# Two joined layers on one core: another order for the parameter stage of the convolution, and for the transposes of x

## The chip, the cores and the metric

The kernel runs on one core of a Trainium2 chip. The time is what the device takes for one execution, in microseconds (us), and a kernel's time is the median of its runs. A core has five engines that run their own queues of instructions in order: TensorE (PE in the profile; its weight loads are shown apart as PEld), VectorE (DVE), ScalarE (ACT), GpSimd (POOL) and SyncE (SP, which here only issues DMA transfers). Engines wait for one another by semaphores.

## The reference

Two layers that share nothing, their outputs side by side.

```
def _A_ref(x, mem0, Wq, Wk, Wv, Wo, seg_len):      # x 2048 x 1024, 32 heads of 128, memory 8 rows, seg_len 32
    mem = mem0
    for s in range(n_seg):                          # 64 segments, one after the other
        h = concatenate([mem, x[segment s]])
        q, k, v = h @ Wq, h @ Wk, h @ Wv            # per head
        p = softmax(where(mask, q @ k.T * scale, -1e9))
        o = (p @ v) @ Wo
        mem = o[:8];  outs.append(o[8:])

def _B_ref(u, A, B, C, log_dt, Dskip):              # u 2048 x 1024, D = 1024 channels, N = 128 states, complex
    dt = exp(log_dt)
    P = exp((dt * A)[:, :, None] * l)               # l = 0 .. 2047
    K = einsum('dn,dnl,dn->dl', C, P, dt * B).real
    y = irfft(rfft(pad(u)) * rfft(pad(K)))[:2048]   # length 4096
    return y + u * Dskip
```

Weights are bf16, x and u too; the output is 2048 x 2048.

## The kernel before, in words

`part_b` computes the second layer, and then `part_a` the first. Part A walks through the 64 segments, each of which needs the memory that the one before gave; it streams most of its weights from memory. What of a segment doesn't depend on the memory is worked out ahead, within part B, by the class `Ahead`: in every segment of 32 rows, the last 8 ("left rows", as they are what is left beside 24) get their keys, queries and values projected there (`projections`, 96 **slices**: 8 matmuls of 128x512 for keys and queries, L169, or 16 of 128x256 for values, L156, out of a transposed copy `xTl` of these rows; a slice ends with an eviction, L178 or L163, and stores to memory). The other 24 rows of a segment are only transposed and stored to `VXd`, for part A to read. Both come from `transposes`: 16 blocks of 128 rows, each loaded on POOL's queue, turned by eight PE transposes (L109) and copied by ACT into two places, the stage for `VXd` (L112) and `xTl` (L113). A slice's weights are 512 KB, loaded by SP into one of four buffers.

Part B's order is written out by hand. Its stages:

- **Parameter stage.** From A, B, C and log_dt, as 128x1024 f32 tiles, come for each state the logarithm of a modulus, a phase and a step's phase, in turns. Each goes to a scratch in memory (`PB`) as a sum of two or three bf16 parts (`put3`). `rows(q)` builds two small tables (RE, RT) on DVE. `matrices` makes the transform matrix MF (16 columns x cosine and sine x 512) by DVE and ACT: an angle by a product, its rounding by adding and subtracting a large number, then ACT's sine. The 16 blocks of x are turned in this stage, and 10 slices run. These pieces are generators, and `run` takes a step of each in turn.
- **Sixteen rounds**, by the string `ORDER`: in a round, eight pa matmuls (L1204) each followed by an exponential on ACT (L1212, E0 to E7), eight ptt matmuls (L1198) each followed by a rounding on DVE (L1220), two sines (L1225), two cosines (L1234), products on DVE (L1186, L1187) and a contraction on PE (L1016) that gives part of the kernel K, put to `Kd`. Beside that, words `P0` to `P5` start a slice, `p0` to `p5` evict it, and `U` words transform u (L975, with MF; its sums and differences on DVE, L986 and L987). ACT changes its function table twice a round. `classes` (L956 to L960) adds and subtracts pairs of those sums on POOL and stores them to `Ud` on POOL's queue. pa has one buffer. u is loaded in four quarters of its channels (`load_uq`), two ahead.
- **A transition**, with `build` (gf, L1137 and L1149; `make` steps it) and `weighted` (L1159), which make the tables of the transform of K.
- **Sixteen blocks** b, each a quarter of the channels (256) by a quarter of the frequencies: `spectrum(b + 1)` on PE (hps, L1175), the product with u's transform on DVE (`pointwise`, L1380 to L1386) into a buffer Bt, four blocks to a buffer. From block 4 on, `inverses` (yp, L1436) runs on PE, two for every block, with `ending` behind it. `load_u` and the loads of `MI`, the inverse's matrices, are on SP's queue. In blocks 1 to 14, `resident` loads those weights of part A that stay on the chip. At block 2, POOL forms a product of four rows with u's first rows (L1515), with the rows in a Bt buffer.

Tiles reuse buffers by tag: `kst` (one buffer of 128 x 8192 bf16, where keys and queries of a half are gathered), `wsl` (4), `B` (Bt, two pools), `mn` (two buffers for the inverse's products).

Of the kernel before, what the change touches and what calls it, by code (L numbers as in the profile page):

```python
# [12 lines left out]
I32 = mybir.dt.int32  # L13
# [61 lines left out]
class Ahead:  # L75
# [19 lines left out]
    def transposes(self, pool, ps, ident):  # L95
        nc = self.nc
        def load(b):
            xb = pool.tile([128, self.Dm], BF16, name="xb", tag="xb")
            nc.gpsimd.dma_start(out=xb[:], in_=self.x[b * 128:(b + 1) * 128, :])
            return xb  # L100
        xbs = [load(b) for b in range(3)]
        yield
        for b in range(self.S // 128):
            if b + 3 < self.S // 128:
                xbs.append(load(b + 3))
            xb = xbs[b]
            pt = ps.tile([128, self.KC, 4, self.SL], BF16, name="pt_x", tag="ptx")
            for kc in range(self.KC):
                nc.tensor.transpose(out=pt[:, kc, :, :].rearrange("p a b -> p (a b)"), in_=xb[:, kc * 128:(kc + 1) * 128], identity=ident[:])  # L109
            yield  # L110
            xst = pool.tile([128, 4, self.KC, self.XM], BF16, name="xst", tag="xst")
            nc.scalar.copy(out=xst[:].rearrange("p s k r -> p k s r"), in_=pt[:, :, :, 0:self.XM])  # L112
            nc.scalar.copy(out=self.xTl[:, :, 4 * b:4 * b + 4, :], in_=pt[:, :, :, self.XM:self.SL])  # L113
            nc.sync.dma_start(out=self.VXd[4 * b:4 * b + 4, :, 256:].rearrange("s p f -> p s f"), in_=xst[:].rearrange("p s k r -> p s (k r)"))
            yield
# [545 lines left out]
ON_DVE = (('p1', 'P', 1), ('p4', 'P', 4), ('u0', 'U', 1), ('u1', 'U', 3), ('m', 'M', 0))  # L661


def part_b(ctx, tc, u, A_re, A_im, B_re, B_im, C_re, C_im, log_dt, Dskip, out_b, ahead, copies, residents, first_state):
# [10 lines left out]
    PB = [dram.tile([PARTS[q], 8, 128, 128], BF16, name="PB%d" % q) for q in range(2)]  # L675
# [27 lines left out]
    with tc.tile_pool(name="b_par", bufs=1) as par, tc.tile_pool(name="b_parh", bufs=2) as parh, tc.tile_pool(name="b_mg", bufs=2) as mg, \  # L703
            tc.tile_pool(name="a_prx", bufs=4) as prx, tc.tile_pool(name="a_ppt", bufs=4, space=PSUM) as ppt:
        ldt = par.tile([128, 8], BF16, name="ldt")
        sy.dma_start(out=ldt[:], in_=log_dt.rearrange("(t p) -> p t", p=128))
        nat = {}
        for nm, src in (("Cr", C_re), ("Ci", C_im), ("Br", B_re), ("Bi", B_im), ("Ai", A_im), ("Ar", A_re)):
            nat[nm] = par.tile([128, 8, N], BF16, name="nat" + nm)
            sy.dma_start(out=nat[nm][:], in_=src.rearrange("(t p) n -> p t n", p=128))  # L710
        dtb = par.tile([128, 8], BF16, name="dtb")
        sc.activation(out=dtb[:], in_=ldt[:], func=ACT.Exp)
        sh = [128, 8, N]

        def f32(name):
            return par.tile(sh, F32, name=name)

        def put3(x, q, row):
            hi = parh.tile(sh, BF16, name="hi", tag="hi")
            sc.copy(out=hi[:], in_=x[:])  # L720
            sy.dma_start(out=PB[q][row].rearrange("t p n -> p t n"), in_=hi[:])
            yield
            v.tensor_tensor(out=x[:], in0=x[:], in1=hi[:], op=ALU.subtract)
            mid = parh.tile(sh, BF16, name="mid", tag="mid")
            sc.copy(out=mid[:], in_=x[:])
            sy.dma_start(out=PB[q][row + 1].rearrange("t p n -> p t n"), in_=mid[:])
            yield
            lo = parh.tile(sh, BF16, name="lo", tag="lo")
            v.tensor_tensor(out=lo[:], in0=x[:], in1=mid[:], op=ALU.subtract)
            sy.dma_start(out=PB[q][row + 2].rearrange("t p n -> p t n"), in_=lo[:])  # L730
            yield

        def run(*gens):
            gens = list(gens)
            while gens:
                for g in list(gens):
                    if next(g, g) is g:
                        gens.remove(g)

        ci = mg.tile([128, 512], I32, name="ci", tag="ci", bufs=1)  # L740
        gp.iota(ci[:], pattern=[[2, 512]], base=1, channel_multiplier=0)
        ri = mg.tile([128, 4, 4], I32, name="ri", tag="ri", bufs=1)
        gp.iota(ri[:], pattern=[[1, 4], [512, 4]], base=0, channel_multiplier=4)
        colk = mg.tile([128, 512], F32, name="colk", tag="colk", bufs=1)
        v.tensor_copy(out=colk[:], in_=ci[:])
        v.tensor_scalar(out=colk[:], in0=colk[:], scalar1=float(1.0 / (2 * PLEN)), scalar2=None, op0=ALU.mult)
        rowl = mg.tile([128, 16], F32, name="rowl", tag="rowl", bufs=1)
        v.tensor_copy(out=rowl[:], in_=ri[:].rearrange("p a b -> p (a b)"))

        def some(g, n):  # L750
            for _ in range(n):
                next(g, None)
                yield

        def sines(c, cs):
            return MF[:, :, c:c + 2, cs, :].rearrange("p k c n -> p c k n")

        def columns(tm):
            return tm[:].rearrange("p c (k n) -> p c k n", k=4)

        def matrices():

            tms, kMs = {}, {}
            for c in range(0, 20, 2):
                if 4 <= c:
                    tm = tms.pop(c - 4)
                    v.tensor_scalar(out=tm[:].bitcast(I32), in0=tm[:].bitcast(I32), scalar1=0x7FFFFFFF, scalar2=None, op0=ALU.bitwise_and)
                    sc.activation(out=sines(c - 4, 0), in_=columns(tm), func=ACT.Sin, scale=-TWO_PI, bias=hp[:])
                if 2 <= c < 18:
                    tm = tms[c - 2]  # L770
                    v.scalar_tensor_tensor(out=tm[:], in0=kMs.pop(c - 2)[:], scalar=MAGIC, in1=tm[:], op0=ALU.subtract, op1=ALU.subtract)
                    sc.activation(out=sines(c - 2, 1), in_=columns(tm), func=ACT.Sin, scale=-TWO_PI)
                if c < 16:
                    tms[c] = mg.tile([128, 2, 512], F32, name="tm", tag="tm", bufs=4)
                    for i in range(2):
                        v.tensor_scalar(out=tms[c][:, i], in0=colk[:], scalar1=rowl[:, c + i:c + i + 1], scalar2=None, op0=ALU.mult)
                    kMs[c] = mg.tile([128, 2, 512], F32, name="mkM", tag="mkM")
                    sc.activation(out=kMs[c][:], in_=tms[c][:], func=ACT.Identity, bias=magic[:])
                yield

        dt_b = dtb[:].unsqueeze(2).to_broadcast(sh)
        mats = matrices()
        for _ in range(2):
            next(mats)


        jI = par.tile([128, NE + NA], I32, name="jI")
        o = 0
        for b0, st, n in FINE + COARSE + TURNS:
            gp.iota(jI[:, o:o + n], pattern=[[st, n]], base=b0, channel_multiplier=0)  # L790
            o += n
        jF = par.tile([128, NE + NA], F32, name="jF")
        v.tensor_copy(out=jF[:], in_=jI[:])
        pI = par.tile([128, 2], I32, name="pI")
        gp.iota(pI[:, 0:1], pattern=[[1, 1]], base=0, channel_multiplier=1)
        v.tensor_scalar(out=pI[:, 1:2], in0=pI[:, 0:1], scalar1=3, scalar2=None, op0=ALU.bitwise_and)
        pF = par.tile([128, 2], F32, name="pF")
        v.tensor_copy(out=pF[:], in_=pI[:])
        tI = par.tile([128, 8], I32, name="tI")
        gp.iota(tI[:], pattern=[[1, 8]], base=0, channel_multiplier=0)  # L800
        tF = par.tile([128, 8], F32, name="tF")
        v.tensor_copy(out=tF[:], in_=tI[:])
# [18 lines left out]
        own, lo, hi_ = rows(0)  # L821
        jE = par.tile([128, NE], F32, name="jE")
        v.tensor_scalar(out=hi_, in0=lo, scalar1=-1.0, scalar2=1.0, op0=ALU.mult, op1=ALU.add)
        v.tensor_scalar(out=jE[:, 0:NF], in0=jF[:, 0:NF], scalar1=lo, scalar2=None, op0=ALU.mult)
        v.tensor_scalar(out=jE[:, NF:], in0=jF[:, NF:NE], scalar1=lo, scalar2=hi_, op0=ALU.mult, op1=ALU.add)
        v.tensor_tensor(out=RE[:], in0=bcast_mid(own[:], NE), in1=bcast_front(jE[:], 8), op=ALU.mult)
        own, lo, hi_ = rows(1)
        jT = par.tile([128, NT], F32, name="jT")
        ang = par.tile([128, 1], F32, name="ang")
        v.scalar_tensor_tensor(out=ang[:], in0=lo, scalar=-1.0, in1=hi_, op0=ALU.add, op1=ALU.add)  # L830
# [80 lines left out]
        for i in range(9):  # L911
            next(mats, None)
            evict_next = next(pro)
            evict((sc.copy, v.tensor_copy)[i % 2])
            evict = evict_next
# [779 lines left out]
```

## Time and profile before

| | |
|---|---|
| median of 3 runs | 2008.63 us (2002.54 to 2014.86) |
| profiled execution | 2001.01 us, of which the span of the profile is 1999.3 us |
| mean granted PE clock | 0.971 |
| busy: PE, DVE, ACT, POOL | 1831.9, 1413.8, 960.1, 416.9 us |
| DMA | 588.69 MB, mean 294 GB/s |
| first exponential of round 0 (L1212) | 103.23 us |
| first sine of rounds 0, 1, 2 (L1225) | 115.80, 135.74, 156.20 us |
| a round after that | 19.95 us |
| first pointwise product (L1380) | 436.09 us |
| first matmul of the inverse (L1436) | 496.80 us |

All times within an execution count from the span's start. A share of busy time is a mean over stages with different limits, so the table of windows, below, is read stage by stage. Matmuls are pipelined and their ends are modelled: a busy PE is not a PE at its peak, and the time from one group's start to the next's says more than a group's length.

### The profile page before, as it was taken

What the parts mean: (1) busy time and instruction counts of PE and PEld (TensorE: products, weight loads), DVE (VectorE), ACT (ScalarE), POOL (GpSimd) and SP (SyncE); (2) the same over time, 40 slices, a digit from 0 to 9 for tenths busy, and PEclk for the clock granted to TensorE, in tenths of its full rate; (3) what the DMA queues carried; (4) which work ended last, traced back from release to release, by engine and by line L of the source; (5) the groups of instructions that cost most, each with busy time, mean ns of one, the idle gap of its engine ahead of it and who ended that gap; (6) DMA issues with size and microseconds to landing.
All of it is one profiled execution on the core that took longest, in us unless ns stands there. A gap on an engine that the chain in (4) does not pass through costs nothing.

```text
span 1999.3 us, 74588 instructions
## 1 busy us (share of the span) xinstructions
PE 1831.9 (92%) x31956; PEld 1131.2 (57%) x31956; DVE 1413.8 (71%) x3441; ACT 960.1 (48%) x1673; POOL 416.9 (21%) x851
## 2 busy tenths in 40 slices
PE   1589999978999799999999999999999999999999
PEld 1365766645888455555555555555555555555554
DVE  8779999988995366666666666666766666666650
ACT  4888989872223243434343434444343444444330
POOL 2126454533100011111111111111111111111120
PEclk9699999977999899999999999999999999999999
DMA  6688997748768999999999999999999999999991
GB/s 173 179 229 266 266 267 204 193 117 278 216 203 260 328 327 340 341 331 349 340 340 335 351 337 342 346 342 349 348 348 342 337 347 340 349 342 349 344 339 42
DMA packets 348484, 588.69 MB, mean 294 GB/s; under 512 B 109880, under 2 KB 225928, under 8 KB 346104
## 3 DMA queue, kind: packets, MB, share of 16 engines
q1 hardware_dynamic: 294764, 526.35, 78.0%
q10 hardware_dynamic: 44812, 28.26, 4.6%
q0 software_dynamic: 8576, 29.32, 4.2%
q8 instruction: 250, 4.10, 0.8%
q14 instruction: 82, 0.67, 0.1%
HBM read 528.25 MB, written 66.05 MB: 297 GB/s over the span
## 4 chain that ended last, share of the span: by engine, by line
PE 39%; DMA 21%; DVE 3%; issue 1%; ACT 1%; POOL 0%; SPq 0%; DVEq 0%; POOLq 0%
PE acc L376 23%; DMA wst<-WD_v 8%; PE pp L489 8%; DMA wst<-WD_o 7%; PE pe L626 3%; PE tr L387 2%; DMA wst<-WD_k 2%; DMA arena<-PKd 2%; DMA wst<-WD_q 2%; PE pv L457 1%; DVE arena L583 1%; PE sc L401 1%; PE pv L461 1%; ACT arena L583 1%; PE tro L589 1%
## 5 line engine op out<-in xcount | busy, mean ns | idle before, releaser
L376 PEld LDWEIGHTS <-a_hT 128*32 128x32 bf16 x12352 | 328.0, 96 | 313.6 <-issue 57.0
L382 ACT CAST arena<-acc 128x512 bf16<-128x512 f32 x384 | 225.1, 586 | 393.9 <-PE acc L376 314.6
L489 PEld LDWEIGHTS <-arena 128*32 128x32 bf16 x8256 | 216.3, 96 | 86.9 <-issue 62.5
L376 PE MATMUL acc<-wst,a_hT 128*32 128x512 bf16 x2304 | 230.2, 382 | 23.9 <-DMA wst<-WD_v 20.5
L390 POOL COPY arena<-arena 128x128 bf16<-128x128 bf16 x128 | 37.3, 292 | 825.0 <-DMA arena<-PKd 277.9
L297 DVE TENSOR_SCALAR arena<-keep 128x256 int32<-128x256 int32 (+1 forms) x512 | 175.7, 395 | 27.6 <-PE acc L376 27.2
L376 PE MATMUL acc<-XM,a_hT 128*32 128x512 bf16 x2560 | 185.9, 381 | 0.0
L169 PE MATMUL pro<-XM,wsl 128*128 128x512 bf16 x512 | 119.5, 389 | 10.4 <-ACT XM L113 8.1
L489 PE MATMUL pp<-W_o,arena 128*32 128x256 bf16 x3584 | 122.8, 274 | 4.7 <-DMA W_o<-in_A_Wo_dram 4.6
L416 DVE TENSOR_REDUCE a_mx<-sc 128x4 f32<-128x160 f32 (+1 forms) x192 | 71.7, 374 | 74.9 <-PE sc L404 74.9
L420 ACT ACTIVATE sc<-sc 128x160 f32<-128x160 f32 (+1 forms) x192 | 63.9, 333 | 125.5 <-DVE sc L417 124.9
L376 PE MATMUL acc<-W,a_hT 128*32 128x512 bf16 x1536 | 119.4, 382 | 0.1
L504 DVE COPY arena<-tr 128x512 bf16<-128x512 bf16 x64 | 27.2, 425 | 126.8 <-PE tr L387 126.8
L424 DVE TENSOR_REDUCE a_mx<-sc 128x4 f32<-128x160 f32 (+1 forms) x192 | 72.8, 379 | 55.5 <-ACT sc L420 55.2
L1212 ACT ACTIVATE E<-pa 128x648 bf16<-128x648 f32 x128 | 91.1, 711 | 29.2 <-PE pa L1204 24.1
L1436 PE MATMUL yp<-Bt,MI 128*128 128x256 bf16 x680 | 104.5, 273 | 0.0
L376 PE MATMUL acc<-g,a_hT 128*32 128x512 bf16 x1024 | 102.6, 382 | 0.0
L451 POOL TENSOR_TENSOR arena<-arena,a_BD 128x128 bf16<-128x128 bf16 x128 | 51.1, 399 | 236.8 <-DVE arena L434 232.4
L583 ACT CAST arena<-pp 128x128 bf16<-128x128 f32 x64 | 17.0, 266 | 160.2 <-DVE arena L583 160.2
L489 PE MATMUL pp<-wst,arena 128*32 128x256 bf16 x1536 | 76.5, 275 | 17.3 <-DMA wst<-WD_o 14.4
L169 PEld LDWEIGHTS <-wsl 128*128 128x128 bf16 x512 | 51.1, 100 | 72.9 <-issue 18.5
L376 PE MATMUL acc<-wq,a_hT 128*32 128x512 bf16 x1024 | 91.4, 382 | 0.0
(338 smaller groups left out, 4100.2 us busy)
## 6 DMA issues: line engine op xcount, KB each, us to landing
wst<-WD_v SPq DMA_DIRECT2D x256, 512.0 KB
wst<-WD_k SPq DMA_DIRECT2D x192, 512.0 KB
wst<-WD_o SPq DMA_DIRECT2D x192, 512.0 KB
wst<-WD_q SPq DMA_DIRECT2D x128, 512.0 KB
Ud<-ux POOLq DMA_DIRECT2D x16, 1024.0 KB, 5.9
wq<-Ud SPq DMA_DIRECT2D x32, 512.0 KB
wsl<-in_A_Wk_dram SPq DMA_DIRECT2D x16, 512.0 KB
wsl<-in_A_Wv_dram SPq DMA_DIRECT2D x16, 512.0 KB
```

The costliest lines, as they stand in the source:

```text
L169: nc.tensor.matmul(a[:], lhsT=w[:, kc, 128 * j:128 * j + 128], rhs=xTl[:, kc, :, :].rearrange("p s k -> p (s k)"), start=(kc == 0), stop=( ...
L297: nc.vector.tensor_scalar(out=out.bitcast(I32), in0=in_.bitcast(I32), scalar1=0, scalar2=None, op0=ALU.bitwise_or)
L376: nc.tensor.matmul(a[32 * g:32 * g + 32, o_:o_ + rhs.shape[1]], lhsT=hT[:, kc, :], rhs=rhs, start=(kc == 0), stop=(kc == KC - 1), tile_pos ...
L382: nc.scalar.copy(out=q, in_=a[:])
L416: nc.vector.tensor_reduce(out=m_, in_=x, axis=AX.X, op=ALU.max)
L420: nc.scalar.activation(out=flat(sc, i), in_=flat(sc, i), func=ACT.Exp, scale=scale)
L424: nc.vector.tensor_reduce(out=m_, in_=x, axis=AX.X, op=ALU.add)
L489: nc.tensor.matmul(po[32 * qt:32 * qt + 32, o_:o_ + rhs.shape[1]], lhsT=oT[:, h % 4, (h % 16) // 4, :], rhs=rhs, start=False, stop=(h == 3 ...
L583: (nc.scalar.copy if j else nc.vector.tensor_copy)(out=osb[:, 128 * j:128 * j + 128], in_=pp[:, 1, 128 * j:128 * j + 128])
L626: nc.tensor.matmul(pe[n][:], lhsT=left[2 * b + hi // 16][:, 128 * (hi % 16):128 * (hi % 16) + 128], rhs=wo[u][:, 1024 * hh + 512 * n:1024 ...
L1212: sc.activation(out=T["E", r, e // 4][:, lo:lo + 8 * NE].rearrange("p (i c) -> p i c", i=2), in_=T.pop(("p", r, e))[:, :, 0:4 * NE], func= ...
L1436: pe.matmul(yp[:, b, :], lhsT=m_[:, b, cs, kc, :], rhs=Bt[:, kc, j, half, c_, :], start=(kc == 0 and cs == 0 and half == 0), stop=(kc == 3 ...
```

## The change

1. **Parameter stage.** It becomes one list of words (`PAR`), worked off in order. Of x only the left rows are read, in four loads, turned 16 segments at a time (words T), and copied into `xTl` by ACT (c) or DVE (C). The angles of MF come from PE: two 7-row tables of small bf16 numbers, turned by 24 transposes, and 32 matmuls of 128x512 (F) whose result is taken as the low 16 bits of a PSUM word, so that ACT's sine (f) reads turns. The modulus goes by logarithm and exponential, and the angle by an arctangent of a ratio; there is no reciprocal. Eight products of 128x1024 are on POOL (Wi1, Wi2, Wi, pr, s1, s6, lo1, lo6). Channels lie on partitions as (p t) in place of (t p), so a partition's piece of a parameter or of PB is 2 KB in one run; loads are split between SP's and ACT's queues. 21 slices (P, evicted on DVE, d, or ACT, e) run here.
2. **Rounds.** From round 3 on, the word P4 does nothing: five slices a round. A quarter of u is asked for one ahead, at the second of the four steps of the quarter before; the second buffer first holds the 7-row tables of the parameter stage.
3. **Transition.** The last `classes` runs on DVE, ahead of the second half of the first spectrum; it was on POOL, at the end.
4. **Half blocks.** The other 24 rows are turned in blocks 1 to 4 of the sixteen: 3, 5, 6 and 2 blocks of 96 rows, behind that block's spectrum. Loads are on POOL's queue, two blocks to a buffer of tag `mn`, two such pairs ahead; a further pair is loaded when a pair's second block has been copied. ACT copies into ten places of a buffer of tag `B`, and SP stores to `VXd`. The four rows of block 2 move to another tile, and `resident` loads start at block 2.

```
+    def left_rows(self):
+        held = self.pool.tile([128, 4, 2048], BF16, name="xl", tag="kst")
...
+            self.nc.gpsimd.dma_start(out=xb, in_=x_s[16 * i:16 * i + 16, self.XM:self.SL, :])
...
+    def other_rows(self, two, stage, bank, ident):
...
+            t_ = two()
+            for i in range(2):
+                b = blocks.pop(0)
+                xb = t_[0:n, 1024 * i:1024 * i + 1024]
+                nc.gpsimd.dma_start(out=xb, in_=x_s[4 * b:4 * b + 4, 0:self.XM, :])
+                xbs.append((b, xb))
+        load()
+        load()
         yield
...
+        while xbs:
+            b, xb = xbs.pop(0)
+            pt = bank()[:, :, 0:n]
             for kc in range(self.KC):
...
+                nc.tensor.transpose(out=pt[:, kc, :], in_=xb[:, 128 * kc:128 * kc + 128], identity=ident[0:n, 0:n])
+            xst = stage()
+            nc.scalar.copy(out=xst.rearrange("p s k r -> p k s r"), in_=pt.rearrange("p k (s r) -> p k s r", r=self.XM))
+            nc.sync.dma_start(out=self.VXd[4 * b:4 * b + 4, :, 256:].rearrange("s p f -> p s f"), in_=xst.rearrange("p s k r -> p s (k r)"))
+            if b % 2 and blocks:
+                load()
             yield
...
+PAR = ("F0 Wr2 T0 T1 T2 F1 f0 T3 F2 c2 C1 c0 Wr1 C3 a2 f1 F3 P0 f2 t1 Wr F4 sq1 d0 Wi1 P1 Wi2 t2 f3 F5 f4 d1 t3 a1 P2 Wi m f5 pr F6 P3 d2 "
+         "sq2 F7 P4 mx f6 d3 sm hi1 P5 d4 P6 f7 p lnm P7 lns q4 d5 ex t4 F8 P8 e6 F9 ra d7 xr at t5 P9 d8 b1 f8 f9 hi2 F10 f10 F11 d9 s1 f11 "
+         "mi1 b2 P10 F12 F13 d10 f12 f13 P11 hi4 b3 F14 d11 F15 P12 q3 F16 f14 hi6 f15 F17 s6 hi3 s4 P13 f16 d12 F18 f17 s3 mi4 F19 lo1 f18 "
+         "d13 P14 s2 mi3 F20 F21 d14 f19 f20 lo3 rt P15 F22 f21 F23 F24 mi6 d15 F25 lo6 f22 mi2 f23 f24 P16 lo4 F26 lo2 rp f25 f26 F27 d16 "
+         "F28 f27 F29 f28 P17 F30 F31 f29 f30 f31 P18 e17 e18 P19 e19 P20 e20").split()
...
+            "Wi1": tt(gp, W_im, nat["Cr"], nat["Bi"], MU), "Wi2": tt(gp, y2, nat["Ci"], nat["Br"], MU), "Wi": tt(gp, W_im, W_im, y2, AD),
...
+            "pr": tt(gp, x3, W_re, W_im, MU), "ra": tt(v, x3, x3, x5, MU), "at": act(x3, x3, ACT.Arctan),
...
+            "rp": powers_rows, "rt": phase_rows}
+        for k, x, eng in (("1", x1, gp), ("2", x2, v), ("6", x6, gp), ("4", x4, v), ("3", x3, v)):
+            par_ops.update({"hi" + k: high(k, x, 0), "s" + k: rest_(eng, k, x), "mi" + k: high(k, x, 1), "lo" + k: lowest(eng, k, x)})
...
+            pe.matmul(mt[:], lhsT=turns_l[:, i // 2, :], rhs=turns_r[:, i % 2, :], start=True, stop=True)
...
+                sc.activation(out=MF[:, :, i // 2, i % 2, :], in_=mt[:].bitcast(I16)[:, 0:1024:2].rearrange("p (k n) -> p k n", k=4), func=ACT.Sin,
+                              scale=float(TWO_PI / 65536))
...
-        uvs = [load_uq(0), load_uq(1)]
+        uvs = [load_uq(0)]
...
+                if kc == 1 and dq < 3:
+                    uvs.append(load_uq(dq + 1))
...
-                            sums.append(lambda: classes(kc, dq, got[2], s_))
+                            sums.append(lambda: classes(v, kc, dq, got[2], s_))
...
+            elif nm == "P4" and f > 2:
+                continue
...
     weighted(0, 1, amps[0])
+    sums.pop()()
     spectrum(0, 1, [t_[:, 0] for t_ in now[1]])
...
+    others = ahead.other_rows(two, stage, lambda: banks[-1](), ident)
+    next(others)
     for b in range(16):
         dq = b // 4
+        if b == 4:
+            for _ in others:
+                pass
...
-            rows4 = bp.tile([128, 4, 2, 2, 2, DQ], BF16, name="r4", tag="B")[0:4, 0, 0].rearrange("p a b c -> p (a b c)")
+            rows4 = g0[0:4, 5120:6144]
...
-        for _ in range({1: 2, 2: 2, 3: 1, 4: 2, 5: 2, 6: 2, 7: 1, 11: 3, 12: 3, 13: 2, 14: 3}.get(b, 0)):
+        for _ in range({1: 3, 2: 5, 3: 6}.get(b, 0)):
+            next(others)
+        for _ in range({2: 1, 3: 2, 4: 3, 5: 3, 6: 2, 7: 1, 11: 3, 12: 3, 13: 2, 14: 3}.get(b, 0)):
             next(resident)
```

Lines that the list leaves out as "..." are the small tables, the products of the parameter stage and the loads of its inputs, which the words above tell.

More of the change, by code (lines that the diff above doesn't have):

```diff
@@ L758, in columns @@
[L758 to L779, printed above, removed]
```

348 lines of the change are left out of this document (177 added, 171 removed).

## The prediction

> **What bounds the kernel now.** I read the page's strip of 40 slices first (50 us each; a digit is the busy share in tenths), to find the stages.
>
> ```profile
> PE   1589999978999799999999999999999999999999
> ...
> DVE  8779999988995366666666666666766666666650
> ACT  4888989872223243434343434444343444444330
> POOL 2126454533100011111111111111111111111120
> PEclk9699999977999899999999999999999999999999
> ```
>
> Slices 1 and 2 are the parameter stage: TensorE (PE) nearly empty, its clock down to 0.6, VectorE (DVE) and ScalarE (ACT) full. Slices 3 to 8 are the sixteen rounds, 9 and 10 the first half blocks, and from slice 11 on PE is full to the end. So a microsecond taken ahead of slice 10 counts whole only if nothing between gives it back. Then the busy times by window (columns: window, length, then PE, weight loads, DVE, ACT and POOL busy with instruction counts, clock, DMA share, GB/s):
>
> ```profile
> 0.00:25.00 25.00, 4.06 (x32) 3.18 (x33) 21.26 (x54) 8.13 (x8) 9.32 (x31) 1.00 0.86 210
> 25.00:50.00 25.00, 3.97 (x32) 3.39 (x32) 22.04 (x17) 15.55 (x19) 2.41 (x4) 0.93 0.54 136
> 50.00:75.00 25.00, 7.23 (x64) 5.93 (x64) 20.19 (x22) 18.91 (x31) 3.98 (x6) 0.57 0.84 210
> 75.00:103.00 28.00, 25.67 (x99) 10.70 (x99) 21.54 (x34) 26.47 (x29) 5.60 (x27) 0.84 0.56 151
> ...
> 254.00:274.00 20.00, 20.00 (x242) 11.61 (x241) 18.68 (x30) 17.91 (x21) 10.22 (x13) 1.00 1.07 275
> ...
> 474.00:497.00 23.00, 17.45 (x124) 13.42 (x124) 22.86 (x21) 1.89 (x4) 10.19 (x32) 0.85 0.84 281
> 497.00:650.00 153.00, 151.80 (x1368) 131.64 (x1367) 126.69 (x149) 46.78 (x52) 7.68 (x20) 1.00 0.72 227
> ```
>
> DVE bounds the parameter stage up to 75 us, ACT and PE after it. The first exponential of the rounds (L1212, "E0" below) starts at 103.23 us. DVE bounds the last of the first half blocks (22.86 of 23). The inverse (yp, L1436) starts on PE at 496.80 and keeps PE full until part A. These two times, **E0 and the inverse's start**, are my yardsticks.
>
> **Parameter stage.** Removed are the 128x1024 products that made the transform's angles on DVE and ACT, a reciprocal of 6.55 us (L885) and 24 of every 32 transposed rows. Left, by rows of this profile:
> - DVE: 23 steps of 128x1024 f32 at 1.14 us (26.2), 2 with a scalar at 0.60, 17 evictions at 0.60 (10.2), 2 PSUM copies at 0.68, the two row builders at 2.45 and 3.3, some 20 small ones at 0.13: 48 us.
> - ACT: 8 functions at about 1.0, 10 casts at 0.95, 32 sines out of PSUM at 0.52 (16.6), five evictions at 0.57, three turn copies at 0.98, two xTl copies at 0.7, some 8 table loads at 1.28: 52 us.
> - PE: 21 slices at 1.73 (24 matmuls took 5.18), 32 angle matmuls at 0.27, 56 transposes at 0.13 cold: 52 us.
>
> Three engines with about 50 us each, against 85 on DVE before. PE's slices can't begin until the left rows are transposed and copied. A load of x lands about 5 us after issue here, and four pieces must be issued, landed, transposed (1.03 each) and copied (0.7): I put the first slice at 14.2, an estimate. From there PE has 36.3 (slices) + 8.6 (angles) + 1.7 (the first slice cold: 64 cold matmuls took 16.61), and about 5 for ptt, table load and pa ahead of E0: 66. The word list delays some slices behind the two row builders on DVE: 70. **Floor of the gain: E0 at 70, −33.**
>
> Eight 128x1024 products go to POOL. This trace shows what that does beside DVE (start, length, engine, line):
>
> ```profile
> 447.88 6.30 DVE L1159 TENSOR_TENSOR XM<-XM 128x1536 bf16<-128x1536 bf16 x1
> ...
> 448.08 1.28 POOL L956 TENSOR_TENSOR ux<-us 128x512 f32<-128x512 f32 x1
> 449.33 1.29 POOL L957 TENSOR_TENSOR ux<-us 128x512 f32<-128x512 f32 x1
> 450.59 2.77 POOL L959 TENSOR_TENSOR ux<-us 128x256 f32<-128x256 f32 x4
> ```
>
> A DVE product that takes 0.95 us elsewhere ends only when POOL's products have ended; at 486.37 an L1383 of 1.22 took 2.38 beside POOL's L1515. By L956, eight of twice its width take 8 x 2.57 = 20.6 us. DVE works in order, so evictions queue behind a blocked product, and PE behind them. With 48 us of work in some 55, DVE takes about half of the 20.6 as delay: E0 at 79, **−24**. All of it would be E0 at 86 to 90, −17 to −13.
> The Trainium skill, "SBUF — State Buffer", section on who interferes with whom, has a VectorE instruction with two SBUF inputs and a GpSimd one that reads SBUF exclude each other for whole instructions. L1159's 6.30 agrees; by that rule alone, all of the 20.6 would be paid only if no other VectorE work were free to run.
>
> The first load of u for the rounds is now behind seven stores on SP's queue, and the first ups matmul of round 0 waits for it; between 0 and 3.8 us, I take **+3.5** (it sits behind the last eviction).
>
> **Rounds.** Twelve rounds lose P4 (8 or 16 matmuls, 1.73 us of PE) and its eviction (0.68 of DVE). What sets a round's 19.95 us is seen on ACT (idle before in brackets):
>
> ```profile
> 272.63 0.71 ACT L1212 ACTIVATE E<-pa 128x648 bf16<-128x648 f32 x1 [0.63 <-PE pa L1204]
> 273.87 0.71 ACT L1212 ACTIVATE E<-pa 128x648 bf16<-128x648 f32 x1 [0.53 <-PE pa L1204]
> 274.60 1.28 ACT L1225 ACT_TABLE_LOAD   x1
> 275.89 1.72 ACT L1225 ACTIVATE sn<-nr 128x1824 bf16<-128x1824 f32 x1
> ```
>
> PE reads 100% busy, but the waits for pa are those of a single pa buffer: exponential, matmul, exponential. P4 stands behind the last pa, beside E7, the table load and the sines. DVE, too, meets the sines with 0.2 us in hand. So I take 0.13 a round, **−1.6**; bounds 0 and the whole 1.73 a round (−21).
>
> **Between rounds and blocks.** The last class products go from POOL to DVE: 2.4 us there by 1.14 for a step of 1024, while DVE has 5 us idle in 418:436. L1159's extra 5.35 goes; PE lost 1.85 right behind it, then 0.54. What is late next is the following coefficient load, at about 447. I take **−2.5** (0 to −5.3).
>
> **The other 24 rows of x in the first half blocks.** Added in blocks 1 to 4, ahead of the inverse: 16 loads on POOL's queue, 128 transposes on PE, 16 copies of 0.69 to 0.81 on ACT, which is idle (1.89 of 23), and 16 stores on SP ahead of the next load of u. PE's queue gets them in order: 24 transposes ahead of the fourth spectrum, 40 ahead of the fifth, 64 ahead of the sixth, then the inverse.
> - Transposes: eight take 0.45 to 0.62 warm and 1.03 cold, so 16 blocks cost 7 to 16.5; I take 10.
> - Loads: two pairs of blocks ahead, a further pair issued only when a pair is used. A pair needs 2 x 0.6 of issue and 5.0 to land. The wait of a pair that was not issued early is about 5 less the transposes beside it. I find two such on PE (blocks 6 and 7, blocks 12 and 13), and POOL's own product (L1515) ahead of the third pair: +10.
> - Stores: SP's loads of u(4) and u(5) queue behind five and eight stores, and Bt of the fifth block reuses the buffer the stores read: +2, with a colder PE:
>
> ```profile
> 486.39 6.21 PE L1175 MATMUL hps<-XM,g 128*128 128x256 bf16 x40 [2.45 <-DVE y L1380]
> 492.43 4.53 PE L1175 MATMUL hps<-XM 128*128 128x256 bf16 x40
> ```
>
> - Cover: PE is idle for 9 us between 436 and 497, and DVE is the bound of its last 23; I credit 4, as most of that idle time lies ahead of where the transposes go.
>
> That is **+18**: 10 + 10 + 2 − 4. The lower bound is 8 (transposes in idle time, one wait), the upper 28 (transposes cold, 16.5; waits 10; 2 for stores, no cover). After the inverse starts PE is full, so none comes back. The weights that part A keeps are loaded one block later: free, as the DMA share there is 0.72.
> The Trainium skill, "TensorE: Matmul & The Clock Gate", Part 4, says that transposes don't count as busy for the clock. The granted 0.57 in 50:75, where PE did little else, agrees. By that rule all three spectra of blocks 3 to 5 would run cold, as rival 3 has them.
>
> **Sum**, against the profiled execution (2001.01 us, span 1999.3, 1.7 around it): −24 + 3.5 − 1.6 − 2.5 + 18 = −6.6, so 1994.4 for one like it. The median shown, 2008.63, is 0.38% above that execution; on its scale **2002**.
>
> **Rivals.**
> 1. *POOL's products find DVE elsewhere and the x rows are mostly covered.* For: eight POOL products in a 60 us stage, DVE evictions read PSUM; against: 6.30 beside 0.95. E0 at 70, rows at +8 to +12: −33 + 3.5 − 1.6 − 2.5 + 10 = −23.6, **1985** in the median's scale. Chance 0.22.
> 2. *PE is the bound of the rounds after all* (it reads 20.00 of 20): 12 x 1.0 to 1.73 off on top of my sum, −17 to −26: **1982 to 1991**. Against: ACT's single-buffer waits. Chance 0.09.
> 3. *Slower: the chain of x loads sets the half blocks.* If each of the six later pairs waits out its 6.2 us on PE's in-order queue (37), with transposes cold (16.5) and the spectra cold too (three of 40 at 8.0 for 4.53, by 20 in 4.02: 10), less 9 of idle: +54, in place of +18: **2038**. It decides from about +44 on, where it outweighs the −24 by 1%. For: two buffers only, loads issued behind POOL's own products; against: the loads are for the next block, and spectra lie between. Chance 0.13.
> 4. *The change doesn't shorten the parameter stage as it says*: DVE blocked for all of 20.6, E0 at 88, −15 in place of −24: **2011**, inside the forecast's band. Chance 0.14.
>
> My own case has 0.42. **Faster by over 1%** (about what a measurement of this kernel can tell from no change: its runs spread by 0.6%): rivals 1 and 2, 0.31. **Slower by over 1%**: rival 3 and 0.01 of rival 4, 0.14. **Within**: the rest, 0.55. The range leaves out the far end of rival 2 and rival 3: downwards −33 + 0 − 1.6 − 2.5 + 8 = −29, and 2 of rival 2's smallest share: 1977; upwards −15 + 3.8 + 0 + 0 + 28 = +17: 2025.
>
> **What would show it.** E0 at 79 (70: rival 1; 88: rival 4), with DVE products of 2 to 4 us beside POOL's. Sines 19.8 us apart (18.5: rival 2). The inverse at about 490, 17 us behind where E0's gain alone puts it (rival 3: over 50), PE waiting for loads of xb in two places. The forecast is most likely wrong in how much of POOL's 20.6 DVE pays, and in how many x loads PE waits for.

## The result, and the profile after

The changed kernel takes **2058.93 us** (median of 4 runs, 2053.86 to 2063.03) against 2005.59 us of the kernel before in the same comparison: a ratio of **1.0264**, 95% interval 1.0227 to 1.0301. It is slower by 53 us, where 2002 was forecast and 2025 was the end of the range. Its profiled execution took 2063.03 us (span 2061.3), the slowest of the four.

The page's strip for the changed kernel (40 slices of 51.5 us, busy share in tenths; last line the DMA engines):

```profile
PE   7699999783599879989999999999999999999999
...
DVE  7499989874399446666766666566666666667650
...
PEclk8899999866699979999999999999999999999999
DMA  6869975646567889999999999999999999999991
```

PE is now busy in the first two slices, as the change wants. The hole has moved to slices 10 and 11, from about 464 to 567 us, which lie in the half blocks. The same by windows (window, length, then PE, weight loads, DVE, ACT, POOL busy with counts, clock, DMA share, GB/s):

```profile
25.00:50.00 25.00, 24.87 (x108) 9.38 (x107) 23.47 (x27) 22.36 (x27) 3.97 (x2) 1.00 0.52 151
...
254.00:274.00 20.00, 18.74 (x275) 14.75 (x274) 17.93 (x30) 17.89 (x21) 9.31 (x12) 1.00 0.91 246
...
480.00:500.00 20.00, 4.51 (x36) 3.30 (x35) 2.21 (x2) 3.20 (x4) 6.02 (x8) 0.50 0.30 77
500.00:520.00 20.00, 6.62 (x56) 5.14 (x54) 6.98 (x6) 2.40 (x3) 1.96 (x3) 0.67 0.72 205
520.00:540.00 20.00, 3.28 (x32) 2.44 (x32) 0.00 (x0) 3.20 (x4) 3.38 (x10) 0.50 0.41 116
```

In the stretch from 480 to 540 no engine is busy for half of the time, and DMA is at 0.30, 0.72 and 0.41: something is being done one at a time. The times that part the stages:

| us from the span's start | before | after | difference | each stage's own |
|---|---|---|---|---|
| first exponential of the rounds, E0 | 103.23 | 83.22 | −20.0 | −20.0 |
| first sine | 115.80 | 101.05 | −14.75 | +5.25 |
| last sine | 418.43 | 405.32 | −13.1 | +1.65 |
| first matmul of the inverse | 496.80 | 549.90 | +53.1 | +66.2 |

From the inverse to the end this execution took 1511.4 us, and before 1502.5. In ten of the eleven edited kernels below that last part took 1496 to 1510, so the 9 us are within what executions differ by (the eleventh, e11 with 1517, has a reason of its own, given there); the 53.1 ahead of it is the whole difference of the medians.

What happened from 480 to 545 is seen when PE's queue and POOL's are laid side by side. PE first (start, length, engine, line, what, idle before and what ended it):

```profile
504.47 0.51 PE L134 MATMUL yp<-b_ident,xb 96*128 96x96 bf16 x8
511.41 0.82 PE L134 MATMUL yp<-b_ident,xb 96*128 96x96 bf16 x8 [6.44 <-DMA xb<-in_A_x_dram]
516.82 0.82 PE L134 MATMUL yp<-b_ident,xb 96*128 96x96 bf16 x8 [4.58 <-DMA xb<-in_A_x_dram]
522.26 0.82 PE L134 MATMUL yp<-b_ident,xb 96*128 96x96 bf16 x8 [4.62 <-DMA xb<-in_A_x_dram]
...
543.83 0.82 PE L134 MATMUL yp<-b_ident,xb 96*128 96x96 bf16 x8 [4.77 <-DMA xb<-in_A_x_dram]
544.45 5.61 PE L1191 MATMUL hps<-XM 128*128 128x256 bf16 x40
549.90 6.71 PE L1453 MATMUL yp<-Bt,MI 128*128 128x256 bf16 x60
```

Every block of rows is waited for by itself, 5.4 us apart, and the spectrum and the inverse stand behind the last of them. And POOL, which issues those loads:

```profile
485.66 0.67 POOL L125 DMA_DIRECT2D xb<-in_A_x_dram  x1 [0.57 <-PE pt_x L134]
490.89 0.68 POOL L125 DMA_DIRECT2D xb<-in_A_x_dram  x1 [4.57 <-issue]
496.61 0.65 POOL L125 DMA_DIRECT2D xb<-in_A_x_dram  x1 [5.04 <-issue]
501.98 0.65 POOL L125 DMA_DIRECT2D xb<-in_A_x_dram  x1 [4.72 <-issue]
...
517.08 0.65 POOL L125 DMA_DIRECT2D xb<-in_A_x_dram  x1 [4.75 <-issue]
```

The load at 490.89 had its buffer (it shares it with the load at 485.66), and no semaphore that it waits for was late: "issue" is a wait that the profile knows no releaser of. A load lands 5.1 us after issue (median), so the next one goes out just as the one before has landed. **One load at a time**, in place of the two pairs that the code holds buffers for.

### The profile page after: what moved, and what is told of

Its sections match the earlier page's. It is cut to its first block, busy times and chain, and to the rows that moved or that the text cites. A ratio compares the mean times of both kernels' runs of the same rounds, so it can differ in the third digit from the quotient of the medians.

```text
span 2061.3 us, 74713 instructions
## 1 busy us (share of the span) xinstructions
PE 1854.4 (90%) x32044; PEld 1136.8 (55%) x32044; DVE 1375.0 (67%) x3407; ACT 956.2 (46%) x1673; POOL 419.7 (20%) x862
## 3 DMA queue, kind: packets, MB, share of 16 engines
q0 software_dynamic: 10944, 29.33, 4.3%
## 4 chain that ended last, share of the span: by engine, by line
PE 53%; DMA 26%; DVE 7%; ACT 7%; issue 4%; POOL 1%; ACTq 0%; SPq 0%; DVEq 0%; POOLq 0%
PE acc L401 21%; DMA wst<-WD_v 9%; PE pp L514 8%; DMA wst<-WD_o 7%; PE yp L1453 5%; PE hps L1191 3%; PE ups L991 3%; DMA wst<-WD_k 3%; PE pe L651 3%; ACT sn L1241 2%; PE tr L412 2%; PE pa L1220 2%; DMA arena<-PKd 2%; DMA out_dram<-arena 1%; ACT E L1228 1%
## 5 line engine op out<-in xcount | busy, mean ns | idle before, releaser
L1236 DVE TENSOR_SCALAR nr<-ptt 128x456 f32<-128x456 int16 x128 | 77.4, 626 | 31.3 <-PE ptt L1214 29.7
## 6 DMA issues: line engine op xcount, KB each, us to landing
wst<-WD_v SPq DMA_DIRECT2D x256, 512.0 KB
wst<-WD_k SPq DMA_DIRECT2D x192, 512.0 KB
wst<-WD_o SPq DMA_DIRECT2D x192, 512.0 KB
wst<-WD_q SPq DMA_DIRECT2D x128, 512.0 KB
wq<-Ud SPq DMA_DIRECT2D x32, 512.0 KB
wsl<-in_A_Wk_dram SPq DMA_DIRECT2D x16, 512.0 KB
wsl<-in_A_Wv_dram SPq DMA_DIRECT2D x16, 512.0 KB
```

What stands on the lines that cost most here:

```text
L1236: v.tensor_scalar(out=T["n", r, e // 4][:, lo:lo + 8 * NT], in0=T.pop(("t", r, e))[:, 0:8 * NT].bitcast(I16)[:, 0:16 * NT:2], scalar1=floa ...
```

## Experiments

All times of stages are from the profiled execution of each run. "Stretch" is the time from the last sine to the inverse's first matmul: 78.4 us before, 144.6 after.

### What makes POOL's loads go one at a time: e1, e2, e7

Another queue (e1), in `other_rows`:

```
-                nc.gpsimd.dma_start(out=xb, in_=x_s[4 * b:4 * b + 4, 0:self.XM, :])
+                nc.scalar.dma_start(out=xb, in_=x_s[4 * b:4 * b + 4, 0:self.XM, :])
```

> The 16 loads of x in the half blocks go out on ScalarE's queue in place of POOL's; nothing else. Theory A (POOL's queue takes only one of these loads at a time: in the changed kernel's trace they are issued 5.0 to 6 us apart, each about when the one before has landed): two pairs are in flight again, the transposes wait only at the ends of pairs, the inverse starts at about 502 us in place of 549.9 (483.7 without any cost of the rows, plus the 18 of the prediction), and the time falls by some 48 us to about 2011. Theory B (what holds the half blocks is PE's cold transposes, the stores on SP or the reuse of two buffers): the inverse starts at 540 to 550, the time stays within 12 us of 2059.

Measured: 2035.22 us, ratio to the kernel before 1.0156 (1.0127 to 1.0185); inverse at 529.1, stretch 122.6. So 22 us of the stretch go, not 48. Part of the rest is the edit's own: the 24 stores of K on SP, which stand ahead of the first block's load of u, took 27.7 us in place of 17.6 in the changed kernel, and VectorE waited 17.2 us for that load (7.2 before the edit). What held the stores is named by the waits of SP's queue in e1 (425 to 450 us: waiter, releaser, sum, times, longest):

```profile
SPq L1047 <- DMA xb<-in_A_x_dram: 11.8, 4, 7.1
```

Four stores waited for the four first loads, with which they share no data; in the trace each of them uses the completion semaphore of one of these loads. In the changed kernel SP has no such wait. The run shows that POOL's queue is at fault, not how much.

Another shape on the same queue (e2): whole blocks of 128 rows, which lie together in memory.

```
-                nc.gpsimd.dma_start(out=xb, in_=x_s[4 * b:4 * b + 4, 0:self.XM, :])
+                nc.gpsimd.dma_start(out=xb, in_=self.x[128 * b:128 * b + 128, :])
```

> The same 16 loads stay on POOL's queue, but each takes a whole block of 128 rows (256 KB in one run of memory) in place of 4 x 24 rows (192 KB); the transposes turn 128 rows, and the copy leaves the left rows out. Theory A1 (what limits POOL's queue is room for a load's packets, and a load of 4 x 24 rows makes some 200 of them, where a load of 128 rows in the kernel before made about 77, three in flight): three loads in flight, the inverse starts at 500 to 510, time 2010 to 2020. Theory A2 (POOL's queue is serial in the half blocks whatever the shape, for instance because VectorE keeps it from writing descriptors): loads still 5 to 6 us apart, the inverse at 545 to 560, time 2055 to 2070.

Measured: **2021.73 us**, ratio 1.0092 (1.0068 to 1.0115); inverse at 514.4, stretch 109.6: 35 us less for more bytes. POOL's queue in that run:

```profile
444.90 1.76 POOL L125 DMA_DIRECT2D xb<-in_A_x_dram  x3 [2.29 <-DMA MI<-MId]
449.19 0.55 POOL L125 DMA_DIRECT2D xb<-in_A_x_dram  x1 [2.53 <-issue]
464.04 1.10 POOL L125 DMA_DIRECT2D xb<-in_A_x_dram  x2 [14.30 <-PE pt_x L134]
```

Three go out back to back, and the fourth waits on "issue". Theory A1 has its sign and most of its size; the inverse is 4 us later than its 510.

Is it the 96 partitions or the four pieces? e7 loads 96 rows that lie together:

```
+                nc.gpsimd.dma_start(out=xb, in_=self.x[n * b:n * b + n, :])
```

> The changed kernel with one edit: a load of 96 rows in the half blocks takes 96 rows that lie together in memory in place of 4 x 24 (so part A gets other rows of x than it should). It stays at 192 KB, 96 partitions and POOL's queue. If the four runs of 24 rows are what makes a load's 208 packets (48 of 4 KB, 144 of 8 bytes, 16 of 4 bytes), there are now about 64, three or four loads in flight, and the inverse starts near 514 as with full blocks. If it is the 96 partitions, the packets stay 208, the loads 5 to 6 us apart, and the inverse starts at 545 to 555.

Measured: inverse at 512.0, stretch 106.4, 2017.27 us in one run. Now four go out together:

```profile
445.69 2.30 POOL L125 DMA_DIRECT2D xb<-in_A_x_dram  x4 [0.48 <-DMA MI<-MId]
464.16 1.07 POOL L125 DMA_DIRECT2D xb<-in_A_x_dram  x2 [16.18 <-PE pt_x L134]
```

The number of packets is on every page, in part 3, in the row of the software queue, which is POOL's (packets, MB, share). In e1, where these 16 loads are not on this queue:

```profile
q0 software_dynamic: 7616, 26.17, 3.7%
```

In the changed kernel:

```profile
q0 software_dynamic: 10944, 29.33, 4.3%
```

With contiguous rows (e7):

```profile
q0 software_dynamic: 8640, 29.32, 4.3%
```

So the 16 loads of 4 x 24 rows make 10944 − 7616 = 3328 packets, 208 each, and the 16 of e7 make 8640 − 7616 = 1024, 64 each, for the same 29.3 MB in all. In e2 the row has 8896: 1280 for 16 loads of 128 whole rows, 80 each (64 of 4 KB and 16 of 4 bytes). In flight at once were 3 x 80 and 4 x 64, and never 4 x 80 or 2 x 208: **the queue holds at least 256 and fewer than 320 packets** in this kernel, and a load of four pieces takes most of that for itself. It is not a limit in bytes: e7 had 4 x 192 KB in flight, and the changed kernel never 2 x 192 KB. The kernel sets the scratch for this queue's descriptors to 512 bytes a partition (`SCRATCH`), in the functions outside the change. No run changed that; that the limit comes from there is argued and not shown.

### The rest of that stage: e8, e11, e5

e8 leaves the rows out, and has the early load of u that is described with e3:

```
-    others = ahead.other_rows(two, stage, lambda: banks[-1](), ident)
+    others = iter(())
```

> Left out: the loads, transposes and copies of the other 24 rows; part A reads other data in their place, stored once a round from SP with the same bytes. The first load of u is early. This is the changed kernel without its fourth part. If the block stage has no other debt than these rows: 78.4 to 81 us from the last sine to the inverse, as before, the inverse at 477 to 481, the time 16 to 20 us below the kernel before. If the other moves (class products on VectorE, weights kept by part A loaded a block later) cost something: over 84.

Measured: 1989.87 us, ratio **0.9917** (0.9894 to 0.994); inverse at 478.2, stretch 79.1. Everything else in the change, with one load moved, is worth 16 us; of the 66.2 that the stretch grew by, 65.5 are the rows.

e11 keeps every transpose, copy and store, and loads only the first four blocks:

```
             if b % 2 and blocks:
-                load()
+                xbs.extend((blocks.pop(0), x_) for x_ in kept[:2])
```

> Full blocks of 128 rows, the early first load of u, and only the first four blocks of other rows are loaded; the other twelve turns read those tiles again, so every transpose, copy and store stays at its place and no transpose waits for a load behind the fourth (part A gets repeated rows). The stretch from the last sine to the inverse was 79.1 us without these rows and 109.6 with all loads of full blocks. If the waits for loads are most of what full blocks still cost: 88 to 95. If transposes on a cold PE, copies and stores are most of it: 100 to 108.

Measured: the inverse starts at 486.7, a stretch of 86.2, below the lower expectation. But it then runs 1516.8 us to the end, 14 more than in e2, and VectorE shows a reason:

```profile
497.20 2.36 DVE L1409 TENSOR_TENSOR Bt<-y 128x1024 bf16<-128x1024 f32 x2 [8.06 <-DMA wq<-Ud]
```

This is block 4's product, which the inverse soon needs; PE waited 5.5 us for VectorE behind it. The profile puts the wait down to a load of u, but the instruction reads no u. It writes Bt of the fifth block, the buffer that the rows' stores read, and SP had issued the last of these stores at 490.5. So here the inverse's start flatters, and the span is the better measure: 2003.5, 17.6 above e8's 1985.9.

e5 tries what is left with full blocks: the POOL product goes behind the loads, and the transposes behind the next load of u.

```
+        for _ in range({2: 3, 3: 5, 4: 9}.get(b, 0)):
+            next(others, None)
...
+        if b == 3:
+            gp.tensor_tensor(out=w4, in0=rows4[:, 0:D], in1=w4, op=ALU.mult)
```

> On top of full blocks of 128 rows on POOL's queue and the early first load of u: the product of four rows on POOL is issued a block later, behind loads of x in place of ahead of them, and the transposes of a block come behind the next block's load of u on SP (PE's order is unchanged). In the run with full blocks the stretch from the last round's first sine to the inverse took 109.6 us, where the kernel before took 78.4: 31 more, with PE waiting 10.8 us for the pair of loads behind POOL's product and VectorE 14.6 and 11 us for loads of u behind stores. If those two queues are the rest of the cost: the stretch takes 88 to 97, the inverse starts at 488 to 497, and the time is that of the kernel before within 8 us. If it is PE's cold transposes and the two buffers themselves: the stretch stays over 103, the time about 2013.

Measured: 2017.47 us, ratio 1.005 (1.0027 to 1.0072); stretch 105.6, the inverse at 506.8. The first expectation falls, and its rival (over 103) came: these two queues were worth 4 us of the 31. VectorE's waits for u were not the cause but followed what PE waited for; with the loads of u ahead of the stores, it waits for PE (8.1 us for a spectrum) and for the stores that leave the buffer of the fifth block (13.5).

By spans of single executions, all with u early: 2045.5 with the loads as they are (e3, below), 2010.3 with full blocks and better queues (e5), 2003.5 with only four loads (e11), 1985.9 without the rows (e8). So of some 60 us, **some 35 are the loads' one-at-a-time issue**; the medians of the changed kernel and of e2 differ by 37. Some 25 remain with full blocks. By these spans, 7 of them are waits for loads that remain, and 18 the transposes, copies and stores themselves in queues that run in order. That division is rough: e5's runs spread over 19 us and its profiled one lies 5 below their median. With the medians of e5 and e8 it is 12 and 15.

### The parameter stage: e3, e4

e3 issues the first load of u from the word list (at P15), not behind the last stores.

```
+            if word == "P15":
+                for r in range(4):
+                    sy.dma_start(out=u_first[:, 4 * r:4 * r + 4, :], in_=u_rows[r][:, :, 0:DQ])
...
-        uvs = [load_uq(0)]
+        uvs = [u_first]
```

> The first load of u for the rounds is issued on SP during the parameter stage (at the word P15, about 64 us) in place of behind the stores of the last slices (88.25 us). If the 5.88 us that E4 of round 0 waited are the landing of that load: the first sine moves from 101.05 to about 95.7 us, E0 stays at 83.2 within 1, and everything up to the half blocks moves by -5. Rival: DMA shared with the slices' weights is the bound, E0 moves back by 2 to 5 and the first sine stays within 1.5 us.

Measured: E0 at 83.4, first sine at **95.35** in place of 101.05, inverse at 542.9 in place of 549.9. What went is this, from ScalarE's timeline of the changed kernel:

```profile
88.05 0.71 ACT L1228 ACTIVATE E<-pa 128x648 bf16<-128x648 f32 x1 [0.53 <-PE pa L1220]
...
95.11 0.71 ACT L1228 ACTIVATE E<-pa 128x648 bf16<-128x648 f32 x1 [5.88 <-PE pa L1220]
```

The exponential has nothing to do with u. But PE's queue runs in order, and its first transform of u, which stands ahead of the next pa, sat there until the load landed:

```profile
92.67 1.87 PE L991 MATMUL ups<-u_h,XM 128*128 128x256 bf16 x8 [4.66 <-DMA u_h<-in_B_u_dram]
```

e4 puts the eight POOL products on VectorE, at the same places:

```
-            "Wi1": tt(gp, W_im, nat["Cr"], nat["Bi"], MU), ...
+            "Wi1": tt(v, W_im, nat["Cr"], nat["Bi"], MU), ...
...
-        for k, x, eng in (("1", x1, gp), ("2", x2, v), ("6", x6, gp), ...
+        for k, x, eng in (("1", x1, v), ("2", x2, v), ("6", x6, v), ...
```

> The eight products of 128x1024 of the parameter stage run on VectorE, at the same places of the word list. Theory (the exclusion of POOL and VectorE costs about as much as it saves: VectorE instructions drawn out beside POOL's sum to 10 to 11 us in the changed kernel): 9 us of products come to VectorE and 10 go; the integer cast of 4.20 us takes under 0.5, Wr1 1.2 in place of 2.76; the first slice starts at about 17.5 in place of 19.4, and E0 is at 83 within 4. Rival (VectorE's 48 us were the bound and the exclusion is hidden): E0 at 90 or later.

Measured: the first slice at 17.81 in place of 19.43, E0 at 83.36 in place of 83.22. VectorE of the changed kernel, beside POOL's products:

```profile
10.07 4.20 DVE L807 CAST jF<-jI 128x106 f32<-128x106 int32 x1 [5.09 <-POOL jI L776]
...
15.93 2.76 DVE L853 TENSOR_TENSOR Wr<-natCr,natBr 128x1024 f32<-128x1024 bf16 x1
...
51.62 3.20 DVE L878 TENSOR_TENSOR x<-x,part 128x1024 f32<-128x1024 f32 x1 [1.36 <-ACT part L873]
...
61.26 2.02 DVE L846 TENSOR_SCALAR RT<-RT,ang 128x456 bf16<-128x456 bf16 x1
```

And the first, second and last of these in e4:

```profile
10.15 1.05 DVE L807 CAST jF<-jI 128x106 f32<-128x106 int32 x1 [5.18 <-POOL jI L776]
...
12.02 1.22 DVE L853 TENSOR_TENSOR Wr<-natCr,natBr 128x1024 f32<-128x1024 bf16 x1
...
61.57 0.34 DVE L846 TENSOR_SCALAR RT<-RT,ang 128x456 bf16<-128x456 bf16 x1
```

The six instructions that POOL drew out in the changed kernel (the four above, one of 1.48 and one of 2.55) lose some 10 us against 1.2 for a product and the e4 rows for the other two. Eight products on VectorE cost about as much. So POOL's eight products bring nothing, and take nothing.

### The rounds: e10, e6, e9

e10 takes out the line that skips P4, so a round has six slices again.

```
-            elif nm == "P4" and f > 2:
-                continue
```

> The changed kernel with P4 in every round again: six slices a round, so that they run out a few rounds earlier. If a round is set by ScalarE and the single pa buffer, the distances of the sines stay at 19.95 to 20.2 with five slices and with six, and the last sine comes within 2 us of 405.3. If PE with six slices were the bound, rounds with five would have been shorter: then they are 1 us or more longer here.

Measured: eleven of the fourteen rounds up to the last but one take 19.94 to 20.22 us, as with five slices; the other three take 22.4, 22.6 and 21.6, and the last sine is at 411.8, 6.5 late. A sixth slice doesn't lengthen a round as such, so PE's matmuls don't set it. The expectation of 2 us for the sum is missed, and the trace of e10 shows why for two of the three long rounds: they are the first two without slices, the last of which ends at 343 us. By windows, the round before and these two:

```profile
323.62:343.56 19.94, 19.94 (x307) 16.26 (x297) 18.61 (x30) 17.84 (x20) 10.17 (x13) 1.00 0.68 183
343.56:366.13 22.57, 13.49 (x229) 8.81 (x220) 18.68 (x30) 15.95 (x17) 10.47 (x13) 0.77 0.87 220
366.13:387.76 21.63, 11.48 (x197) 7.67 (x196) 17.58 (x28) 15.95 (x16) 9.31 (x12) 0.76 0.28 107
```

PE was idle for 8.6 and 9.6 us in one piece, and then ran at a lower granted clock: eight transforms of u took 1.91 us at 354 and 1.03 at 361, and ScalarE waited up to 1.9 us for a pa. In the changed kernel slices last until 370 us, the clock in these two rounds is 1.00, and they take 19.95 us each. So leaving out P4 did something that its count of matmuls doesn't show: it made the slices last into these two rounds. What lengthened the third (22.4) was not settled.

If P4's place is free, the rows can be turned there. e6 does that for 12 blocks, with full blocks and u early:

```
+            elif nm == "P4" and f > 2:
+                pending["P", 4] = next(turned_rows)
...
-        for _ in range({1: 3, 2: 5, 3: 6}.get(b, 0)):
+        for _ in range({1: 3, 2: 1}.get(b, 0)):
```

> On top of full blocks and the early first load of u: 12 of the 16 blocks of other rows are turned in the rounds, one in each from the fourth on, at the place that P4 left empty (eight transposes on PE, the copy on VectorE at the place of p4, loads and stores on SP), and only four in the half blocks (three behind block 1, one behind block 2). My account (rounds are set by ScalarE and the single pa buffer, PE has the 1.7 us of P4 to spare): rounds stay at 19.95 to 20.1, the last stretch takes 80 to 85 in place of 144.6 in the changed kernel, the inverse starts at 479 to 485, and the time is 12 to 18 us below the kernel before, about 1988. Rival (DMA, at a share of 0.91 to 1.07 in a round, is what the rounds can't spare): rounds grow by 0.5 to 1 us, and the time is that of the kernel before within 6 us.

Measured: **2002.09 us**, ratio **0.9979** (0.9961 to 0.9998, 12 runs). The stretch is 82.2, as expected; but the rounds take 314.2 us in place of 304.3. Two of them are long, 27.0 and 23.0 us. For the first, ScalarE's timeline shows the reason; the second was not settled:

```profile
171.97 0.71 ACT L1260 ACTIVATE E<-pa 128x648 bf16<-128x648 f32 x1
177.66 0.59 ACT L215 CAST vst<-pro 128x512 bf16<-128x512 f32 x1 [4.98 <-DMA PVd<-vst]
```

To make room for a block of rows, e6 had cut the buffers of staged values from six to four. e9 gives them back and lets the block share another buffer (it also loads it later):

```
-            xb = pool.tile([128, self.Dm], BF16, name="xb", tag="xb")
+            xb = pool.tile([128, 2, 4, 128], BF16, name="xb", tag="ms")[:].rearrange("p a b c -> p (a b c)")
...
+            if 3 <= f < 15 and word == "E2":
+                ahead.load_row()
```

> The kernel with 12 blocks of rows turned in the rounds once more, with six buffers for the staged values again (that run had four, and ScalarE waited 5.0 us for one of them in one round, which grew from 20 to 27 us; another grew to 23); the loaded block shares the buffer of the turned matrices, which is free for most of a round. If those two rounds were the buffers' cost: sixteen rounds take 303 to 306 us from the first sine to the last, as before, in place of 314.2; the inverse starts at 483 to 488; the time is 12 to 17 us below the kernel before. If it is the stores of the rows on SP's queue: the rounds stay over 310 and the time within 6 us of the kernel before.

Measured: 2012.33 us, ratio 1.0043 (1.0017 to 1.0068); the rounds take 326.5, where 303 to 306 was expected. The wait for values is gone and a worse one has come, as the waits of that run show (PE, from 100 to 400 us: waiter, releaser, sum, times, longest):

```profile
PE pt_x L157 <- DMA xb<-in_A_x_dram: 21.5, 5, 9.9
```

SP's queue holds the load behind stores, and PE, in order, waits in five rounds. e6 stays the best of those that do the whole work: 2.8% below the changed kernel, and 0.2% below the kernel before, too little to call it faster.

## Why the prediction was wrong, point by point

- **Parameter stage, −24 forecast, −20.0 measured.** The mechanism and its size were right: some 10 us of VectorE lost to POOL's products. What was too early by 5.2 us is the first slice (14.2 forecast, 19.43 measured). The fourth load of left rows went out 4.4 us late, on the same "issue" as the loads above, and the cast of 4.20 us held VectorE. That this late start is the missing 4 us is argued and not shown: in e4 the first slice came 1.6 us earlier, and E0 did not move. The Trainium skill, "SBUF — State Buffer", section on who interferes with whom, counts copies, casts and products with a scalar among the VectorE instructions that can exclude GpSimd; the cast and L846 agree, 4.20 and 2.02 where e4 has 1.05 and 0.34. I had counted only products of two tiles.
- **First load of u, +3.5 forecast, +5.25 measured**, outside the bounds of 0 to 3.8, for which the prediction shows no row; e3 shows that it was that load.
- **Rounds, −1.6 forecast, +1.65 measured**: 1.4 of it is the last round (24.27 us, 22.83 before), and a round with five slices takes 19.95 as one with six did. So the gain of 0.13 a round was nothing. That PE's slices don't set a round was right, as e10 bears out; that ScalarE and the single pa buffer do is read from waits, and no run changed them.
- **Class products, −2.5 forecast**: the drawn-out L1159 went (6.30 before, 0.95 now), but block 1's first product came 38.3 us behind the last sine, and 35.7 before. Ahead of it VectorE now waits 7.18 us for u. The sentence that named this load as late next was right, and the gain beside it was not: e8, without the rows, has a stretch of 79.1, and the kernel before 78.4.
- **Other rows, +18 forecast, about +65 measured.** The step that failed is the one called "Loads": "two pairs of blocks ahead", a pair needing "2 x 0.6 of issue and 5.0 to land", and only two waits on PE. It took what the code has buffers for as what the queue can hold. Each load waited for the one before, so eleven waits stood where two were counted (PE's weight loads waited 57.2 us in 11). The terms beside it were too small as well: they add up to 8 (10 for transposes, 2 for stores, −4 of cover), and with only four loads 15 to 18 us are left. The stores, put at 2, have a part in that: VectorE waited 8.1 us in e11 and 13.5 in e5 for the buffer that they read. How much each of these terms is worth stays open. The wait on POOL's product and the stores ahead of u were there, but with the loads mended they are worth 4 us.
- **Rival 3** ("the chain of x loads sets the half blocks", +54, 2038, chance 0.13) came nearest, and by 21 us too low in time, of which 12 are rows. Its mechanism, a pair waiting out its 6.2 us, was half of the real one: 5.4 for each load.

The trace of before held a sign, but a weak one. Its code keeps four buffers for x and asks for a fourth load before the first block is used; POOL's queue says when it went:

```profile
5.50 1.86 POOL L99 DMA_DIRECT2D xb<-in_A_x_dram  x3
11.14 0.55 POOL L99 DMA_DIRECT2D xb<-in_A_x_dram  x1 [3.78 <-DMA xb<-in_A_x_dram]
```

Three together, and the fourth as the first lands, though its buffer had never been used. I had read this row for a load's 5.0 us to land, not for how many can be under way. It doesn't show the queue's own limit, as in this trace POOL waits there for the semaphore of the first load. The changed kernel's parameter stage shows it: its four loads of left rows (80 packets each) wait for no semaphore, three have gone out by 4.0 us, and the fourth follows at 8.43

```profile
8.43 0.55 POOL L101 DMA_DIRECT2D xl<-in_A_x_dram  x1 [4.41 <-issue]
```

## What to carry to other kernels

When loads are moved to a queue, count the packets that one of them makes there and see in the trace how many such loads were ever in flight at once: a load of a few short pieces can make several times the packets of a longer one in one piece, and cost more. What is put ahead of a critical matmul on an engine that works in order costs its wait for data and not its own time; eight transposes of under 1 us cost 5.4. A stage that starts earlier moves everything behind it, the loads too: look which queue each of them is now behind.

## What the runs showed that I had not expected

- POOL's DMA queue in this kernel holds 256 packets, and not 320 (3 x 80 and 4 x 64 in flight, not 4 x 80 or 2 x 208).
- A load of 4 x 24 rows of 2 KB makes 208 packets, of which 144 are of 8 bytes; 96 rows in one run make 64, and 128 rows 80.
- A cast of 128x106 elements took 4.20 us beside POOL's products, and 1.05 without.
- In e1, four stores on SP's queue waited 11.8 us for loads on ScalarE's queue with which they share no data but, in the trace, the completion semaphores.
- In e10 the slices ran out at 343 us in place of 370, PE was left idle, and at a granted clock of 0.77 and 0.76 the next two rounds took 22.6 and 21.6 us in place of 19.95.
